# Shifting the SBUF pools of an attention and expert-layer kernel by 64 to 224 bytes

## The chip, the core and the metric

The kernel runs on one core of one Trainium2 chip. The metric is the device time of one execution in microseconds. Three timed runs of the kernel before gave 777.49, 779.59 and 781.82 us; their median, 779.59 us, is the time before.

## What is computed

Two steps follow each other. The first is block-sparse attention over 4 batches, 8 heads, 768 positions and head size 64: a query block of 32 positions sees its neighbours, the first and last block, and three sampled blocks; the first and last query blocks see all.

```python
scores = np.where(mask, scale * q @ k.T, -1e9)
attn = softmax(scores)              # over the keys
x = (attn @ v)                      # 3072 tokens x 512 features
h = x @ w_in                        # 512 -> 2048
g = s * np.maximum(h, 0) ** 2 + b
out = g @ w_out                     # 2048 -> 512
```

The weights arrive as 64-bit floats, and the two matrix products of the second step are done in three single-precision passes each (high by high, high by low, low by high), so that they come out in full precision.

## The kernel before, in words

**Attention.** 52 slots of work (44 for query blocks that see a window and three sampled blocks, 8 for the first and last blocks, which see all: the dense slots) are put in an order by a planner (class `Plan`), which simulates the engines with given costs; the order is then fixed in the program, and nothing is decided at run time apart from the addresses of sampled blocks. A slot runs through scores (lines 921 and 943), minimum and mask (960), exponential (972), transposes by TensorE (998 and 1000), their copies to SBUF (1011 on VectorE, 1013 on ScalarE), the products with the values (1042 and 1052), a scaling (1058), a transpose back (1064), a copy (1069) and a store to DRAM (1077). Keys `kt` are loaded at the start in pieces of 512 bytes per partition and block (692), values `vA` and `vB` in pieces of 2048 bytes (758 to 771 and 865), queries `qr` at line 706, on the queue of SyncE for dense slots and of GpSimd for the others.

**Decoding the weights.** Each 64-bit weight tile is split into a high and a low single-precision tile by nine steps on VectorE and ScalarE (lines 79 to 89). This runs beside the attention and the first part of the second step.

**Expert layer.** Groups of 384 tokens are taken one after the other. The first two groups use plain products (lines 432 to 434: 12 matmuls of 384 columns for each group of 128 hidden features). The other six go by Strassen's scheme, two groups at a time: line 611 issues six matmuls of 384 columns for each product, seven products in place of eight. The hidden values are squared, split into high and low (line 453 on GpSimd), and multiplied by `w_out` (lines 474 to 476: nine matmuls of 512 columns for each group of hidden features).

Every matmul has its own weight load. In lines 432 to 434 and 611 the weights come from the tiles `win` or `wop`, and the moving operand is `xp` (or a tile laid over `wout` or `win`). In lines 474 to 476 the weights are `hid` and the moving operand is `wout`, `woutr` or `win`.

**Where the tiles lie.** A tile pool is a stretch of each SBUF partition; pools that are opened one after the other lie one behind the other. From the bottom: `cpool` (constants), `kp` (`kt`, `kk`, `win`, `raw`, the work tiles of the decoding, the sums), `gp` (`vA`, `vB`, `wout`, `dp`, `xp`), `cp` (`ptile`, later `hid`), and above them the pools that attention alone uses (`pers`, `qp`, `ptp`, `sm` and another one named `xp`). When attention is over, the pool `wo` (`woutr`, `xrest`, `ob`) is laid over those. In `kp`, `gp` and `cp` every tile is a multiple of 512 bytes long, so that all of them have the same place modulo 512 in their partitions.

Of the kernel before, what the change touches and what calls it, by code (L numbers as in the profile page):

```python
# [9 lines left out]
F32 = mybir.dt.float32  # L10
# [9 lines left out]
P = 128  # L20
# [186 lines left out]
def kernel(  # L207
# [42 lines left out]
    cpool = ctx.enter_context(tc.tile_pool(name="cpool", bufs=1))  # L250
# [4 lines left out]
    b_top = cpool.tile([P, 1], F32, name="b_top")  # L255
    nc.gpsimd.memset(b_top, F32_MOST + F64_SHIFT)
    b_most = cpool.tile([P, 1], F32, name="b_most")
    nc.gpsimd.memset(b_most, F32_MOST)
    xd = dpool.tile([B // 2, 2, P, NM, 2, NPAIR, BLK], F32, name="xd")
    wod = dpool.tile([4, P, 2 * DM], F32, name="wod")  # L260
# [16 lines left out]

    gp = ctx.enter_context(tc.tile_pool(name="gp", bufs=2))
    cp = ctx.enter_context(tc.tile_pool(name="cp", bufs=1))

    ptiles = [cp.tile([P, HALF], F32, tag=f"p{n}", name=f"ptile{n}") for n in range(8)]
    ps = ctx.enter_context(tc.tile_pool(name="ps", bufs=1, space=PSUM))

# [18 lines left out]
    wts, wos, moved = {}, {}, {}  # L302
# [16 lines left out]
    def win_tile(k):  # L319
        if k not in wts:  # L320
            wts[k] = kbig(k, f"win{k}").rearrange("p n a c -> p (n a c)") if k < 2 else kp.tile([P, 14 * NW], F32R, tag="kk", name="win2", bufs=1)
        return wts[k]
# [11 lines left out]
    def wos_tile(k):  # L334
        if k not in wos:
            pair = wos[("pair", k // 2)] = gp.tile([P, 2, 4 * DM], F32R, tag="vg", name=f"wout{k}", bufs=2)
            wos[k // 2 * 2], wos[k // 2 * 2 + 1] = pair[:, 0], pair[:, 1]
        return wos[k]

    def wout(f, part):  # L340

        if f in moved:
            return moved[f][part]
        if f < 2:
            return win_tile(0)[:, (8 + 2 * f + part) * NW:(9 + 2 * f + part) * NW]
        if f < 8:
            o = (2 * (f % 2) + part) * DM
            return wos_tile(f // 2)[:, o:o + DM]
        if "rest" not in wos:
            es.close()  # L350
            wos["pool"] = ctx.enter_context(tc.tile_pool(name="wo", bufs=1))
            wos["rest"] = wos["pool"].tile([P, NFC - 9, 2, DM], F32R, name="woutr")
            wos["x"] = wos["pool"].tile([P, HALF], F32, name="xrest")
        if f == NFC - 1:
            return win_tile(2)[:, (10 + part) * NW:(11 + part) * NW]
        return wos["rest"][:, f - 8, part, :]
# [106 lines left out]
    def mlp2(i, gf=None):  # L463
        g, f = gf or subs[i]
        gh, gl = htile(2 + i % 3), htile(5 + i % 3)
        b, hf = divmod(g, 2)
        count[g] = count.get(g, 0) + 1
        first, last = count[g] == 1, count[g] == NFC
        for t in range(TG):
            if first:  # L470
                po[(g, t)] = bank(2 + 3 * hf + t, f"o{g}_{t}")
            acc = po[(g, t)]
            tsl = slice(t * P, (t + 1) * P)
            nc.tensor.matmul(acc, gh[:, tsl], wout(f, 0), start=first, stop=False)  # L474
            nc.tensor.matmul(acc, gh[:, tsl], wout(f, 1), start=False, stop=False)  # L475
            nc.tensor.matmul(acc, gl[:, tsl], wout(f, 0), start=False, stop=last)  # L476
            if last:
                ob = wos["pool"].tile([P, DM], F32, tag="ob", name=f"ob{g}_{t}", bufs=3)
                if t % 2 == 0 or b < B - 1:
                    nc.scalar.copy(ob, acc)  # L480
                else:
                    nc.vector.tensor_copy(ob, acc)
                tok = BLK + hf * G + t * P
                if tok + P <= S:
                    nc.sync.dma_start(out=out[b * S + tok:b * S + tok + P, :], in_=ob)
                else:
                    nc.sync.dma_start(out=out[b * S + tok:(b + 1) * S, :], in_=ob[:P - BLK])
                    nc.sync.dma_start(out=out[b * S:b * S + BLK, :], in_=ob[P - BLK:])
# [1060 lines left out]
```

## Time and profile before

| | |
|---|---|
| median of the three timed runs | 779.59 us |
| span of the profiled execution | 784.0 us |
| TensorE busy | 742.1 us, 95% |
| VectorE busy | 581.4 us, 74% |
| ScalarE busy | 472.9 us, 60% |
| GpSimd busy | 248.5 us, 32% |
| moved by DMA | 89.41 MB |

The profiled execution gives no other time of its own than its span, from its first to its last instruction. It lies 4.4 us above the median of the timed runs. Busy time is the sum over the instructions of an engine; a long busy time alone doesn't say that the engine sets the end, for that the chain of waits is read.

### The profile page before, as it was taken

What the parts mean: (1) busy time and instruction counts of PE and PEld (TensorE: products, weight loads), DVE (VectorE), ACT (ScalarE), POOL (GpSimd) and SP (SyncE); (2) the same over time, 40 slices, a digit from 0 to 9 for tenths busy, and PEclk for the clock granted to TensorE, in tenths of its full rate; (3) what the DMA queues carried; (4) which work ended last, traced back from release to release, by engine and by line L of the source; (5) the groups of instructions that cost most, each with busy time, mean ns of one, the idle gap of its engine ahead of it and who ended that gap; (6) DMA issues with size and microseconds to landing.
All of it is one profiled execution on the core that took longest, in us unless ns stands there. A gap on an engine that the chain in (4) does not pass through costs nothing.

```text
span 784.0 us, 21344 instructions
## 1 busy us (share of the span) xinstructions
PE 742.1 (95%) x8032; PEld 625.6 (80%) x8032; DVE 581.4 (74%) x1436; ACT 472.9 (60%) x1141; POOL 248.5 (32%) x395
## 2 busy tenths in 40 slices
PE   8899798998698999999989999999999999999997
PEld 6477675666576889988878888888889888989996
DVE  4657366888687699999898678787668678666652
ACT  3667476788587677778764344475554467445443
POOL 4746244434421232221322223232322223222321
PEclk9889899999899999999999999999999999999999
DMA  9978888756774544544632321125000022000002
GB/s 241 232 199 223 220 218 235 188 159 188 192 198 137 143 133 144 161 142 132 143 114 69 113 75 61 55 54 161 1 1 1 0 61 81 1 1 0 1 1 80
DMA packets 101110, 89.41 MB, mean 114 GB/s; under 512 B 50192, under 2 KB 79504, under 8 KB 101008
## 3 DMA queue, kind: packets, MB, share of 16 engines
q1 hardware_dynamic: 98704, 81.76, 37.2%
q0 software_dynamic: 2304, 6.29, 3.3%
q8 instruction: 63, 1.03, 0.6%
q14 instruction: 39, 0.32, 0.2%
HBM read 69.15 MB, written 14.68 MB: 107 GB/s over the span
## 4 chain that ended last, share of the span: by engine, by line
PE 66%; DVE 16%; ACT 5%; DMA 5%; issue 5%; SPq 2%; POOL 1%; ACTq 0%; POOLq 0%; DVEq 0%
PE m L611 21%; PE o L475 8%; PE o L476 8%; PE o L474 8%; PE s L943 6%; PE xs L1052 5%; PE t L1000 5%; DMA xd<-xst 2%; PE od L1042 2%; DVE win L89 1%; PE xs L1064 1%; DMA qr_3s<-in_q_dup_dram 1%; DVE wout L89 1%; DVE wkhp L88 1%; DVE wklp L82 1%
## 5 line engine op out<-in xcount | busy, mean ns | idle before, releaser
L453 POOL TENSOR_TENSOR hid<-hid,hid 128x384 fp32r<-128x384 f32 x122 | 134.7, 1105 | 369.5 <-ACT hid L629 269.1
L628 ACT ACTIVATE hid<-hid,sb_b,sb_s 128x384 f32<-128x384 f32 x96 | 68.0, 709 | 152.6 <-DVE hid L622 152.6
L972 ACT ACTIVATE ptile<-ptile,nm 128x256 f32<-128x256 f32 (+1 forms) x208 | 107.3, 518 | 44.1 <-DVE nm L960 43.7
L960 DVE CUSTOM_DVE_ANT_1 ptile<-s,mt 128x256 f32<-128x256 f32 x176 | 64.4, 421 | 35.2 <-PE s L943 34.1
L476 PE MATMUL o<-woutr,hid 128*128 128x512 f32 x168 | 66.4, 395 | 0.0
L475 PE MATMUL o<-woutr,hid 128*128 128x512 f32 x168 | 66.3, 395 | 0.0
L611 PE MATMUL m<-wout,win 128*128 128x384 f32 x264 | 62.8, 342 | 3.0 <-ACT xrest L1442 3.0
L474 PE MATMUL o<-woutr,hid 128*128 128x512 f32 x168 | 65.3, 389 | 0.0
L611 PE MATMUL m<-xp,wop 128*128 128x384 f32 x288 | 59.2, 341 | 0.0
L1000 PE MATMUL t<-ident,ptile 128*128 128x128 f32 x352 | 53.0, 296 | 4.9 <-issue 4.8
L1052 PEld LDWEIGHTS xs<-vA,pt 128*32 128x32 f32 x1696 | 36.0, 114 | 26.3 <-issue 10.5
L475 PE MATMUL o<-win,hid 128*128 128x512 f32 x144 | 56.8, 394 | 0.0
L622 DVE SCALAR_TENSOR_TENSOR hid<-hid 128x384 f32<-128x384 f32 x96 | 54.2, 564 | 3.3
L611 PE MATMUL m<-xp,win 128*128 128x384 f32 x288 | 54.8, 337 | 1.2 <-DVE sum L1451 0.8
L1052 PE MATMUL xs<-vA,pt 128*32 128x64 f32 x1696 | 48.1, 228 | 6.5 <-issue 6.3
L611 PEld LDWEIGHTS m<-xp,wop 128*128 128x128 f32 x288 | 52.3, 191 | 2.1
L611 PEld LDWEIGHTS m<-xp,win 128*128 128x128 f32 x288 | 51.0, 188 | 3.8 <-issue 1.1
L629 ACT CAST hid<-hid 128x384 fp32r<-128x384 f32 x96 | 49.4, 515 | 7.3
L882 POOL COPY kk<-kt 128x256 f32<-128x256 f32 (+2 forms) x46 | 20.6, 451 | 104.2 <-PE s L943 104.2
L611 PEld LDWEIGHTS m<-wout,win 128*128 128x128 f32 x264 | 47.8, 189 | 5.7 <-ACT xrest L1442 3.9
L476 PE MATMUL o<-win,hid 128*128 128x512 f32 x126 | 49.9, 396 | 1.7 <-POOL hid L453 1.7
L1000 PEld LDWEIGHTS t<-ident,ptile 128*128 128x128 f32 x352 | 41.0, 149 | 12.1 <-issue 6.3
(188 smaller groups left out, 1867.9 us busy)
## 6 DMA issues: line engine op xcount, KB each, us to landing
vB<-in_v_dram SPq DMA_DIRECT2D x109, 128.0 KB, 3.9
vA<-in_v_dram SPq DMA_DIRECT2D x72, 128.0 KB, 4.1
raw_o<-in_w_out_dram SPq DMA_DIRECT2D x14, 512.0 KB, 3.3
raw_i<-in_w_in_dram SPq DMA_DIRECT2D x12, 512.0 KB, 3.8
xd<-xst SPq DMA_DIRECT2D x44, 128.0 KB, 3.6
out_dram<-ob SPq DMA_DIRECT2D x20, 256.0 KB, 2.0
sum<-xd SPq DMA_DIRECT2D x12, 384.0 KB, 4.4
kt<-in_k_blk_dram SPq DMA_DIRECT2D x8, 384.0 KB, 5.6
```

The lines of the kernel that those rows point to most:

```text
L453: (eng or nc.vector).tensor_tensor(out=htile(5 + i % 3), in0=t, in1=gh.bitcast(F32), op=ALU.subtract)
L474: nc.tensor.matmul(acc, gh[:, tsl], wout(f, 0), start=first, stop=False)
L475: nc.tensor.matmul(acc, gh[:, tsl], wout(f, 1), start=False, stop=False)
L476: nc.tensor.matmul(acc, gl[:, tsl], wout(f, 0), start=False, stop=last)
L611: nc.tensor.matmul(to, w_, x_, start=(c == 0 and k == 0), stop=(c == 1 and k == 2))
L622: vec.scalar_tensor_tensor(out=t, in0=t, scalar=0.0, in1=t, op0=ALU.max, op1=ALU.mult)
L628: nc.scalar.activation(t, t, AF.Identity, bias=sb_b, scale=sb_s)
L629: nc.scalar.copy(gh, t)
L960: nc.vector.tensor_tensor_reduce(out=pt, in0=sp, in1=msk, scale=-scale, scalar=FMAX if g == 0 else nm[:, 0:1], op0=ALU.add, op1=ALU.min, a ...
L972: nc.scalar.activation(pt[:, :w], pt[:, :w], AF.Exp, bias=nms[n][:, last:last + 1], scale=-1.0, accum_out=dns[i][:, g, j:j + 1])
L1000: nc.tensor.transpose(tp[:, (2 * j + c) * P:(2 * j + c + 1) * P], src[:, c * P:(c + 1) * P], ident)
L1052: nc.tensor.matmul(xs[quads[pair]], pt[:, c, quads[pair]], vt[:, a, col:col + D], start=(j == 0 and c == 0), stop=(c == 1), tile_position= ...
```

## The change

Three small tiles are allocated that no instruction writes or reads. One of 64 bytes per partition closes `cpool`, one of 64 bytes opens `gp`, one of 96 bytes opens `wo`.

```diff
@@ -255,6 +255,7 @@
     b_top = cpool.tile([P, 1], F32, name="b_top")
     nc.gpsimd.memset(b_top, F32_MOST + F64_SHIFT)
     b_most = cpool.tile([P, 1], F32, name="b_most")
+    cpool.tile([P, 16], F32, name="shift0")
     nc.gpsimd.memset(b_most, F32_MOST)
@@ -277,7 +278,7 @@
     gp = ctx.enter_context(tc.tile_pool(name="gp", bufs=2))
     cp = ctx.enter_context(tc.tile_pool(name="cp", bufs=1))
-
+    gp.tile([P, 16], F32, name="shift1", bufs=1)
     ptiles = [cp.tile([P, HALF], F32, tag=f"p{n}", name=f"ptile{n}") for n in range(8)]
@@ -349,6 +350,7 @@
             wos["pool"] = ctx.enter_context(tc.tile_pool(name="wo", bufs=1))
+            wos["pool"].tile([P, 24], F32, name="shift3")
             wos["rest"] = wos["pool"].tile([P, NFC - 9, 2, DM], F32R, name="woutr")
```

On every engine the same instructions stand in the same order as before, with the same waits; their addresses in SBUF alone differ. Addresses in PSUM and DRAM stay. The places of the tiles in their partitions, in bytes modulo 512:

| tiles (pool) | before | after | moved by |
|---|---|---|---|
| `kt`, `kk`, `win`, `raw`, `wkhp`, `wklp`, `sum`, `wop` (`kp`) | 256 | 320 | 64 |
| `vA`, `vB`, `wout`, `dp`, `xp` (`gp`) | 256 | 384 | 128 |
| `ptile`, `hid` (`cp`) | 256 | 384 | 128 |
| `ident` (`pers`) | 256 | 384 | 128 |
| `qr` (`qp`), `pt` (`ptp`), `xss`, `xst` (`xp`) | 192 | 320 | 128 |
| `mz` / `mt` (`pers`) | 480 / 224 | 96 / 352 | 128 |
| `woutr`, `xrest`, `ob` (`wo`) | 256 | 480 | 224 |

So the weights `win` and the moving `xp`, which had the same place before, are now 64 bytes apart, and the weights `hid` and the moving `woutr` 96 bytes; `hid` and `wout` still have the same place.

## Rows read from the trace of the kernel before

**Rows 1.** Stages: from:to us, length, busy us (instructions) by engine, clock, DMA share, GB/s.
```profile
0.00:50.00 50.00, 44.41 (x524) 29.88 (x524) 27.51 (x99) 26.49 (x79) 30.26 (x82) 0.86 0.93 225
...
100.00:200.00 100.00, 91.38 (x2340) 65.05 (x2339) 78.27 (x297) 76.13 (x241) 46.05 (x106) 0.97 0.74 200
...
300.00:400.00 100.00, 96.22 (x471) 86.22 (x471) 94.44 (x151) 77.28 (x141) 23.36 (x19) 0.98 0.48 144
...
500.00:600.00 100.00, 99.81 (x496) 89.55 (x495) 74.58 (x149) 56.34 (x116) 28.67 (x26) 1.00 0.18 49
...
700.00:784.00 84.00, 78.89 (x388) 70.02 (x386) 46.00 (x96) 34.57 (x71) 20.07 (x20) 0.99 0.05 20
```

**Rows 2.** The chain that ended last, shares of the span by engine and by line.
```profile
PE 66%; DVE 16%; ACT 5%; DMA 5%; issue 5%; SPq 2%; POOL 1%; ACTq 0%; POOLq 0%; DVEq 0%
PE m L611 21%; PE o L475 8%; PE o L476 8%; PE o L474 8%; PE s L943 6%; PE xs L1052 5%; PE t L1000 5%; DMA xd<-xst 2%; PE od L1042 2%; DVE win L89 1%; PE xs L1064 1%; DMA qr_3s<-in_q_dup_dram 1%; DVE wout L89 1%; DVE wkhp L88 1%; DVE wklp L82 1%
```

**Rows 3.** Timeline of TensorE from 560.7 us: start, length, matmuls merged by line.
```profile
560.74 1.23 PE L611 MATMUL m<-xp,wop 128*128 128x384 f32 x6
561.81 0.39 PE L474 MATMUL o<-woutr,hid 128*128 128x512 f32 x1
...
563.89 2.26 PE L611 MATMUL m<-xp,win 128*128 128x384 f32 x12
565.99 0.39 PE L474 MATMUL o<-wout,hid 128*128 128x512 f32 x1
```

**Rows 4.** The same view at 377.6 us, where 512-column matmuls follow one another.
```profile
377.59 0.39 PE L474 MATMUL o<-woutr,hid 128*128 128x512 f32 x1
...
379.63 0.39 PE L474 MATMUL o<-woutr,hid 128*128 128x512 f32 x1
```

**Rows 5.** Whole span, matmuls and weight loads of lines 611, 474 and 432, in this order.
```profile
0.00:784.00 784.00, 195.00 (x1008) 180.52 (x1008) 0.98 0.41 114
...
0.00:784.00 784.00, 149.60 (x384) 72.30 (x384) 0.98 0.41 114
...
0.00:784.00 784.00, 43.60 (x128) 24.04 (x128) 0.98 0.41 114
```

**Rows 6.** Groups by form: line, engine, out<-in, shapes, count | busy us, mean ns | idle before.
```profile
L1000 PE MATMUL t<-ident,ptile 128*128 128x128 f32 x352 | 53.0, 296 | 4.9 <-issue 4.8
...
L1011 DVE COPY pt<-t 128x512 f32<-128x512 f32 x44 | 30.1, 683 | 10.3 <-PE t L1000 9.8
L1013 ACT COPY pt<-t 128x512 f32<-128x512 f32 x44 | 25.7, 585 | 21.9 <-PE t L1000 21.9
...
L1064 PE MATMUL xs<-ident,xss 128*128 128x128 f32 x88 | 18.5, 293 | 6.0 <-DVE xss L1058 6.0
...
L480 ACT COPY ob<-o 128x512 f32<-128x512 f32 x22 | 12.1, 588 | 7.3 <-PE o L476 5.7 <-DMA out_dram<-ob 1.2
...
L482 DVE COPY ob<-o 128x512 f32<-128x512 f32 x2 | 1.4, 691 | 6.4 <-PE o L476 4.3 <-DMA out_dram<-ob 2.2
```

**Rows 7.** Line 611 at 564.06 and 564.59 us: duration ns min/median/max, first and last start.
```profile
L611 PE MATMUL m<-xp,win x2: 333/336/339, 563.9 to 564.1; 128*128 128x384 f32 x2
...
L611 PE MATMUL m<-xp,win x2: 339/341/343, 564.4 to 564.6; 128*128 128x384 f32 x2
```

**Rows 8.** Single microseconds at the start, columns as in group 1.
```profile
5.00:6.00 1.00, 1.00 (x6) 1.00 (x6) 0.84 (x4) 0.00 (x0) 0.78 (x2) 1.00 1.15 347
...
8.00:9.00 1.00, 1.00 (x11) 1.00 (x10) 0.00 (x0) 0.00 (x0) 0.78 (x3) 1.00 1.09 306
...
13.00:14.00 1.00, 0.81 (x6) 0.22 (x4) 0.85 (x5) 1.00 (x5) 0.00 (x0) 1.00 1.14 344
```

**Rows 9.** Line 89 of the decoding: duration ns min/median/max, first and last start.
```profile
L89 DVE SCALAR_TENSOR_TENSOR win<-wklp,wkhp x17: 691/693/1526, 145.9 to 384.0; 128x512 fp32r<-128x512 f32 x17
L89 DVE SCALAR_TENSOR_TENSOR wout<-wklp,wkhp x8: 693/1392/1523, 272.0 to 315.0; 128x512 fp32r<-128x512 f32 x8
L89 DVE SCALAR_TENSOR_TENSOR woutr<-wklp,wkhp x7: 691/1382/1533, 323.9 to 377.7; 128x512 fp32r<-128x512 f32 x7
```

## The prediction

> **What bounds the kernel now.** I read the stages first. In the first 50 us the DMA engines are busy 0.93 of the time and no other engine is full; from 100 us on TensorE is, with 91 of 100 us, later 96 and 99.8; between 300 and 400 us VectorE stands beside it with 94.44 of 100 [rows 1]. The chain of waits says the same in shares: TensorE holds 66% of it, VectorE 16%, ScalarE 5%, DMA 5%, and of TensorE's part line 611 and lines 474 to 476 make 45 points [rows 2]. So the kernel is bound by TensorE's pace in its second two thirds, by VectorE's decoding in part of the middle, and by transfers at the start. Nothing idles there that a shorter wait could fill. A change of places can move the time only if one of these three runs at another pace at another place.
>
> **What the change removes, adds and moves.** No instruction is added, removed or moved on any queue, and no wait. The term "instructions" of the sum is 0 us. Left is one term for each engine: its instructions at the new places against the old ones. The trace never shows the big tiles at 320, 384 or 480 modulo 512, so each term is bounded by operations that it shows at two other places, 192 and 256, one of them off the 256-byte grid.
>
> ScalarE: the copy of 128x512 numbers from PSUM takes 585 ns into `pt` (at 192) and 588 ns into `ob` (at 256) [rows 6]. The difference is 3 of 588 ns, 0.5%, in either direction. On ScalarE's 5% of the chain, 39 us of 784, that is ±0.2 us.
>
> VectorE: the same copy takes 683 ns into `pt` and 691 ns into `ob` (two instances only) [rows 6], 1.2%. On 16% of the chain, 125 us, that is ±1.5 us; I take 0, because 44 instances against two are no measured difference.
>
> TensorE in attention: a transpose of 128x128 takes 296 ns with its weights in `ptile` (at 256) and 293 ns with them in `xss` (at 192) [rows 6]. The moving operand is `ident` both times, so the distance between the two operands' places is 0 in one case and 64 bytes in the other, the distance that `win` and `xp` get. That is 1%, but these matmuls are short and of another kind than those below, and a conflict could hide in them.
>
> TensorE in the expert layer, the term that matters. In some products the low part of the moving operand is read in runs of 128 bytes with a step of 256, the first half of it from place 256 on, the second from 384 on. Each of the two rows holds one of them and the matmul still running before it. At 564.06 us the first kind starts and is the longer of its row, 339 ns; at 564.59 us the second starts and is the shorter, 339 ns [rows 7]. So a moving operand that starts at 384 and touches other places than its weights goes at the same pace as one that starts at 256. I take 0 for the whole term, since this is the nearest row: same line, same type, same columns.
>
> Its bounds come from the pace itself. Nine matmuls of 512 columns take 563.89 - 561.81 = 2.08 us when they follow a product of line 611 [rows 3], and 379.63 - 377.59 = 2.04 us when they follow others of their kind [rows 4]. A product of six matmuls of 384 columns takes 561.81 - 560.74 = 1.07 us after such a run, two in a row 565.99 - 563.89 = 2.10 us [rows 3], so the second takes 1.03. After each change of kind the pace is thus 0.04 us lower for one group. If that is a conflict between weight loads and moving reads, and it vanishes, the gain is 3 x 384 / 9 = 128 runs of nine (three lines of equal count) times 0.04 = 5.1 us; and for 1008 / 6 = 168 products, half of them first in a row, and 128 / 4 = 32 groups of the plain products, 116 in all, times 0.04 = 4.6 us [rows 3 to 5]. Together 9.7 us is the bound below. A bound much further down: in 2.04 us for nine, one matmul takes 226.7 ns, while 512 columns at the granted clock of 1.00, that is 2.4 GHz, need 213.3; if the 13.3 ns were conflict too, on 1008 + 3 x 384 + 3 x 128 = 2544 matmuls [rows 5] they are 34 us. Bound above: every first group's delay also strikes the other 84 products (3.4 us), and the runs of nine lose as much again as they do now (5.1 us): 8.5 us.
>
> What the Trainium skill says here. "TensorE: Matmul & The Clock Gate", section "Step-by-step: what each phase is for", gives TensorE two independent read ports, so that loading the next weights takes nothing from the running matmul; by it the term is 0 wherever the tiles lie, and the time 779.6 us, as I take it. The same page, section "Back-to-back issue gap", gives N/2.4 + 2.5 ns, 215.8 ns for 512 columns; the trace has 226.7 [rows 4] and differs, so 10.9 ns for each matmul are without an explanation, some 28 us over 2544, and the two-port rule isn't proved by this case.
>
> GpSimd: nothing shows it at another place. It is busy 20 to 30 of 100 us from 300 us on [rows 1] and 1% of the chain [rows 2], so a few per cent of its pace cost nothing; it counts only through VectorE (below).
>
> DMA: queries `qr` land at place 192, keys at 256, both in pieces of 512 bytes. Pure key traffic runs at 347 GB/s between 5 and 6 us; with the order of issue, the queries fall roughly into 8 to 9 us and 13 to 14 us, where 306 and 344 GB/s pass [rows 8]. Against the higher one the loss is 1%, against the lower one 12%. DMA's 5% of the chain is 39 us, so 0.4 to 4.7 us. I take 0, the nearer row being the second, where no key load is left to mix in. A gain would need the grid of 192 to be better than that of 256, which no row shows.
>
> Sum: 0 + 0 + 0 + 0 + 0 us on the profiled execution's 784.0 us. That one lies 4.4 us above the median of the timed runs, so the forecast is set on the median: 779.59 + 0, rounded to 779.5 us. Runs of before differ by ±2.2 us, so about 0.5%, 3.9 us, is what can be told from no change.
>
> **The rivals.**
>
> *TensorE gets smoother.* All operands of a matmul start at the same place modulo 512 now, and after the change `win` and `xp` are 64 bytes apart, `hid` and `woutr` 96. If the 0.04 us for each change of kind come from both reads meeting in one place, they go. For it speaks that the delay is regular and no other engine is named as its cause; against it the two 339 ns [rows 7], and that the delay is absent in rows 4 at unchanged distances. Price: 9.7 us less what VectorE's 94% between 300 and 400 us hides, about a sixth: -8 us, 771.5 us.
>
> *TensorE gets rougher.* The same mechanism turned round: today's equal places keep the two reads out of step, and 64 bytes bring them together. The place is the second product in a row and every run of nine, the price up to 8.5 us: 788 us. It decides from 1.5 ns for each of the 2544 matmuls on (3.9 us). It has the same evidence against it, and rows 4 show that a run at equal places can be free of the delay, so there is something to lose.
>
> *Transfers into SBUF get slower.* Destinations move off the 256-byte grid (320 and 384). With the 12% of rows 8 on DMA's 39 us of the chain the time is +4.7, 784.3 us. It decides from 10% on. Beside it stands the page "DMA: Bandwidth & Descriptors", section "How a descriptor splits into AXI transactions": a descriptor that doesn't start on 256 bytes costs beats for the part before its start. By it pieces of 512 bytes at 320 would take 18 beats for 16, those of 2048 at 384 would take 68 for 64. The 344 GB/s of rows 8 for pieces at 192 don't bear it out, the 306 might.
>
> *VectorE and GpSimd meet otherwise.* Line 89 takes 691 to 693 ns alone, and up to 1533 [rows 9]. Over 693 ns the eight with a median of 1392 hold 8 x 0.70 = 5.6 us, the seven with 1382 hold 7 x 0.69 = 4.8, and of the 17 with a median of 693 fewer than half can hold up to 0.83 each, 0 to 6.7: 10.4 to 17.1 in all, about 13. If small shifts of phase change which of them meet GpSimd's line 453, half of it comes or goes, ±6.5 us: 773 or 786 us. Against it: nothing shifts the phase unless another term isn't 0.
>
> **How the numbers follow.** No change: 0.50. Smoother TensorE: 0.29. Rougher: 0.09. Slower transfers: 0.07. Another phase: 0.05, half to either side. Faster by over 0.5% is 0.29 + 0.02 = 0.31, slower 0.09 + 0.07 + 0.03 = 0.19, within 0.5% 0.50. The evidence for no change comes from neighbouring places, not from the new ones, which is why half is left to the others, and more of it below, where the removable 13.3 ns lie. The likeliest case alone spans 775.7 to 783.5 us. The range reaches past the smoother case in full (779.6 - 9.7 = 770) to 768, which takes in a little of the 34 us, and above to 787, short of the rougher case's end: 768 to 787 us.
>
> **What would show it.** Right: runs of nine at 2.08 and 2.04 us, products at 1.07 and 1.03, copies at 585 to 588 and 683 to 691 ns, and 340 to 350 GB/s between 5 and 8 us. Smoother or rougher would show in the same two timeline views first, long before the stages; slower transfers in the first 50 us, as a later first product with the values; another phase in the durations of line 89 alone. The forecast is wrong if TensorE's stage from 500 to 600 us, 496 matmuls in 100 us now [rows 1], holds 3 matmuls more or fewer.

## The result and the profile after

The changed kernel is slower: 786.81 us median (783.23 to 790.63, 12 runs) against 781.05 for the kernel before, timed beside it (777.49 to 783.22, 12 runs). The medians lie 5.8 us apart; the ratio is 1.0082, 95% interval 1.0057 to 1.0107. A second series gave 787.65 (7 runs) against 781.79, ratio 1.0120 [1.0083, 1.0157]. The ratios here and below are taken from the runs of the chip's faster state and not from the medians; two of the twelve runs of `v_first` are left out as slow. The forecast was 779.5 and no change.

The two profiled executions don't show it in their spans: 784.1 us after, 784.0 before. That one of before was among its kernel's slowest; TensorE stands still once for 4.3 us at 206 us, and over the stretch from 204 to 221 us every other execution profiled here is 2 to 5 us quicker. So the timed runs decide how much, and the profile is read for where. The chain of before has (start, length, released by):

```profile
205.99 4.34 issue
```

The stages of after, with single microseconds behind them; columns are those of [rows 1]:

```profile
0.00:50.00 50.00, 38.30 (x406) 25.89 (x410) 24.50 (x88) 23.33 (x69) 27.85 (x77) 0.84 0.96 208
100.00:200.00 100.00, 91.81 (x2421) 65.66 (x2406) 80.27 (x304) 77.24 (x247) 46.66 (x109) 0.98 0.78 205
...
500.00:600.00 100.00, 99.82 (x496) 89.35 (x495) 74.04 (x148) 56.21 (x117) 29.18 (x27) 1.00 0.21 49
...
5.00:6.00 1.00, 1.00 (x6) 1.00 (x6) 0.83 (x4) 0.00 (x0) 0.78 (x2) 1.00 1.15 329
8.00:9.00 1.00, 1.00 (x11) 1.00 (x10) 0.00 (x0) 0.00 (x0) 0.78 (x3) 1.00 1.18 280
13.00:14.00 1.00, 1.00 (x16) 0.61 (x12) 0.85 (x3) 0.00 (x0) 0.00 (x0) 0.73 1.17 290
```

In the first 50 us the DMA engines are busier than before (0.96 for 0.93) and move less (208 GB/s for 225): 10.4 MB for 11.25. The missing 0.85 MB are 4.1 us at 208 GB/s, and TensorE gets through 406 matmuls for 524 [rows 1]. That is one execution: the second profile of the same kernel has 217 GB/s and 548 matmuls in these 50 us, so neither the 4.1 us nor the 406 measures the kernel. The rate of the loads while keys pass is what returns in every profile (below). At 13 us the DMA engines move 290 GB/s for 344 [rows 8]. The stage from 500 to 600 us is as it was, 496 matmuls.

The time from issue to landing (last column, us) in the first 40 us, first before, then after:

```profile
kt<-in_k_blk_dram SPq DMA_DIRECT2D x8, 384.0 KB, 5.6
...
qr_0d<-in_q_edge_dram SPq DMA_DIRECT2D x4, 128.0 KB, 5.1
qr_4s<-in_q_dup_dram POOLq DMA_DIRECT2D x4, 128.0 KB, 7.0
```
```profile
kt<-in_k_blk_dram SPq DMA_DIRECT2D x8, 384.0 KB, 6.8
...
qr_0d<-in_q_edge_dram SPq DMA_DIRECT2D x4, 128.0 KB, 6.4
qr_4s<-in_q_dup_dram POOLq DMA_DIRECT2D x4, 128.0 KB, 9.1
```

Keys and queries land 1.2 to 2.1 us later. The first 25 us of before, v_qr, v_128, after and after_again (v_qr and v_128 are described in the next section; in the first two kernels the keys lie on 256 bytes, in the others off them):

```profile
0.00:25.00 25.00, 22.22 (x172) 17.13 (x176) 13.66 (x45) 12.62 (x34) 14.86 (x47) 1.00 0.95 240
0.00:25.00 25.00, 20.35 (x156) 15.74 (x156) 13.11 (x42) 11.52 (x31) 14.86 (x47) 0.93 0.95 244
0.00:25.00 25.00, 20.13 (x145) 15.30 (x146) 11.30 (x37) 10.31 (x27) 14.78 (x47) 0.86 0.99 213
0.00:25.00 25.00, 20.24 (x145) 14.97 (x146) 11.30 (x37) 10.28 (x27) 14.88 (x47) 0.93 0.98 213
0.00:25.00 25.00, 20.13 (x148) 15.13 (x149) 11.59 (x37) 10.46 (x29) 14.87 (x47) 0.93 0.98 217
```

From 5 to 8 us, before and after:

```profile
5.00:8.00 3.00, 3.00 (x17) 3.00 (x17) 0.84 (x4) 0.00 (x0) 2.41 (x7) 1.00 1.15 346
5.00:8.00 3.00, 3.00 (x21) 3.00 (x21) 0.83 (x4) 0.00 (x0) 2.41 (x7) 1.00 1.16 303
```

TensorE's expert layer does change its cadence, but in both directions. The timeline of after at the places of [rows 3], then of [rows 4]:

```profile
560.30 1.20 PE L613 MATMUL m<-xp,wop 128*128 128x384 f32 x6
561.34 0.39 PE L476 MATMUL o<-woutr,hid 128*128 128x512 f32 x1
...
563.45 2.26 PE L613 MATMUL m<-xp,win 128*128 128x384 f32 x12
565.54 0.40 PE L476 MATMUL o<-wout,hid 128*128 128x512 f32 x1
```
```profile
375.93 0.39 PE L476 MATMUL o<-woutr,hid 128*128 128x512 f32 x1
...
378.03 0.39 PE L476 MATMUL o<-woutr,hid 128*128 128x512 f32 x1
```

Six matmuls after a run of nine take 561.34 - 560.30 = 1.04 us for 1.07, nine after a product 563.45 - 561.34 = 2.11 for 2.08, nine after their kind 378.03 - 375.93 = 2.10 for 2.04.

### The profile page after: what moved, and what is told of

It reads as the page before. It is cut to its first block, busy times and chain, and to the rows that moved or that the text cites. A ratio compares the mean times of both kernels' runs of the same rounds, so it can differ in the third digit from the quotient of the medians.

```text
span 784.1 us, 21344 instructions
## 1 busy us (share of the span) xinstructions
PE 737.6 (94%) x8032; PEld 623.0 (79%) x8032; DVE 582.1 (74%) x1436; ACT 472.7 (60%) x1141; POOL 249.0 (32%) x395
## 4 chain that ended last, share of the span: by engine, by line
PE 78%; issue 6%; DMA 5%; DVE 4%; POOL 3%; ACT 3%; SPq 1%; POOLq 0%; ACTq 0%; DVEq 0%
PE m L613 21%; PE o L476 11%; PE o L478 11%; PE o L477 11%; PE xs L1054 5%; PE s L945 4%; PE t L1002 4%; PE h L434 3%; PE h L435 3%; PE h L436 3%; PE od L1044 2%; DMA qr_3s<-in_q_dup_dram 1%; POOL kk L895 1%; PE xs L1066 1%; DVE whole L580 1%
## 5 line engine op out<-in xcount | busy, mean ns | idle before, releaser
L477 PE MATMUL o<-win,hid 128*128 128x512 f32 x144 | 57.0, 396 | 0.0
L478 PE MATMUL o<-win,hid 128*128 128x512 f32 x126 | 50.0, 397 | 1.0 <-POOL hid L455 1.0
L476 PE MATMUL o<-win,hid 128*128 128x512 f32 x126 | 49.8, 395 | 0.3 <-ACT ob L482 0.2
```

## The experiments

**Two benches of places.** The first loads into one tile at chosen places (its core: `t = big[:, off // 4:...]`, then the DMAs of keys, values and queries); the second runs the expert layer's groups of six and nine matmuls from tiles at chosen places.

> Computes nothing: it only loads into one tile at chosen places modulo 512 bytes, one stretch for each place, and writes zeros. Keys come in pieces of 512 bytes (places 256, 256, 0, 32, ... 480, and 256, 320, 192, 0 again), pairs of keys in pieces of 1024, values in pieces of 2048, queries in pieces of 512 into 64 partitions at a time, then stores. Theory 'destinations off a grid are slower': keys pass at 340 to 350 GB/s at places 0 and 256, as the profile of before has them, and at about 290 at 320, as the profile of after has them; the places between tell which grid it is (64, 128 or 256 bytes); pieces of 2048 lose a quarter as much as those of 512, 4 to 5%. By the page on descriptors the loss at 320 would be 18 beats for 16, 340 to 303. Rival 'the slow start has another cause' (more transfers in flight at once, another order of arrival): all places pass at the same rate within 3%.

A stretch from the middle of each: place 0, 32, 224, 320 with pieces of 512 bytes, then 0 and 192 with pieces of 1024 (columns after from:to: length, VectorE, GpSimd, clock, DMA share, GB/s):

```profile
31.00:38.00 7.00, 0.93 (x6) 0.00 (x0) 1.00 1.14 342
41.00:48.00 7.00, 0.84 (x6) 0.00 (x0) 1.00 1.14 288
105.00:112.00 7.00, 0.84 (x6) 0.00 (x0) 1.00 1.21 290
128.00:135.00 7.00, 0.81 (x6) 0.00 (x0) 1.00 1.16 290
...
231.00:237.00 6.00, 0.46 (x3) 0.00 (x0) 1.00 1.09 386
258.00:264.00 6.00, 0.46 (x3) 0.00 (x0) 1.00 1.09 348
```

It is a step, not a slope: on the 256-byte grid (0 and 256) 332 to 345 GB/s and 27.1 to 27.4 ns for a piece of 512 bytes, at each of the thirteen places off it 288 to 292 GB/s and 31 to 34 ns, 32 and 64 bytes off as much as 128 or 224. Pieces of 1024 take 46.0 ns on the grid and 50 to 52 off it. Queries alone through SyncE's queue, 64 partitions at a time, pass at 195 to 216 GB/s everywhere, and don't care. In the Trainium skill, page "DMA: Bandwidth & Descriptors", section "How a descriptor splits into AXI transactions", a descriptor off the grid pays for the bytes between the boundary and its start, which are fetched and not used. Worked out from that as an estimate, a piece of 512 takes 17 beats for 16 at 32 and 23 for 16 at 224. Here it is the destination that is off the grid; the direction agrees, the amount doesn't: both places cost the same 18 to 19% in time.

> Computes nothing of use: groups of six matmuls of 384 columns and runs of nine of 512, in the expert layer's order (six, six, nine), from tiles that lie at chosen places; first weights at 256 and moving operand at 256 plus 0, 32, ... 480, then both at 0, 64, 128, 192, then the places of before (all 256) and of after (320 and 384 for the products, 384 and 480 for the runs of nine). Theory 'the pace depends on the distance of the two operands': after a run of nine the first six take 1.065 us at distance 0 and 1.045 at 64, nine take 2.08 us at distance 0 and 2.10 at 96, and the numbers repeat by distance, not by the places themselves. Rival 'the pace does not depend on places': all stretches agree within 0.003 us for each group.

TensorE's timeline at distance 0, then at distance 64 (start, length, merged by line):

```profile
63.74 2.24 PE L259 MATMUL bank<-xbig,wbig 128*128 128x512 f32 x9
65.83 2.27 PE L251 MATMUL bank<-xbig,wbig 128*128 128x384 f32 x12
67.93 2.24 PE L259 MATMUL bank<-xbig,wbig 128*128 128x512 f32 x9
```
```profile
97.30 2.22 PE L259 MATMUL bank<-xbig,wbig 128*128 128x512 f32 x9
99.36 2.24 PE L251 MATMUL bank<-xbig,wbig 128*128 128x384 f32 x12
101.44 2.22 PE L259 MATMUL bank<-xbig,wbig 128*128 128x512 f32 x9
```

Nine take 2.081 us at distance 0 (moving less weights) and 2.060 at 64; the first six of twelve 1.066 and 1.040. At 32 and from 96 to 224 nine take 2.087 to 2.106. All repeats after 256 bytes, and with distance 0 it is the same at 0, 64, 128, 192, 256 and 320: the distance counts, not the place. With the places of the changed kernel the first six take 1.037, nine 2.098. The theory held; of its numbers 1.045 was too high. But a group's own distance isn't all. In one stretch the products keep their distance of 0 and only the runs of nine get 96:

```profile
534.66 2.24 PE L251 MATMUL bank<-xbig,wbig 128*128 128x384 f32 x12
536.74 2.26 PE L259 MATMUL bank<-xbig,wbig 128*128 128x512 f32 x9
538.84 0.33 PE L251 MATMUL bank<-xbig,wbig 128*128 128x384 f32 x1
```

The twelve take 2.08 us for the 2.10 beside runs at distance 0, their first six 1.040 for 1.066. Turned round, runs at 0 beside products at 64 take 2.076 for 2.081. So the neighbours' places count too.

**Parts of the change, and its terms kept apart.** All these kernels have the instructions of before, one for one; only places differ. The edits, each on the kernel before:

```
v_first      after b_most:  cpool.tile([P, 16], F32, name="shift0")
v_second     after gp:      gp.tile([P, 16], F32, name="shift1", bufs=1)
v_128        after b_most:  cpool.tile([P, 32], F32, name="shift0")
v_grid       after vA, vB:  gp.tile([P, 16], F32, name="apart", bufs=1);  wo: [P, 24] first
v_qr         after ident:   pers.tile([P, 16], F32, name="shift2")
v_apart      cp made ahead of gp;  after vA, vB: gp.tile([P, 16], F32, name="apart", bufs=1)
v_apart_128  v_apart and v_128 together
v_best       cp, kk, khp, klp behind sb_b; then b_top, b_most, the rest; shift2
```

> Only the first of the three small tiles: everything moves by 64 bytes, so that keys, values, win, hid and wout lie at 320, the queries at 256, and the operands of a matmul keep their distance of 0. Theory 'transfers' (keys at 320 cost the 5 us of the first 50): pure key traffic at 290 GB/s, ratio of after to before 1.004 to 1.007; TensorE's groups as before (1.066, 2.08 us). Rival 'TensorE's pace is the whole loss': ratio 1.000 within 0.002. Rival 'phase': anything from 0.992 to 1.008 with transfers and groups as before.

> Only the second small tile: keys and win stay at 256, values, xp, hid and wout move to 320, queries to 256. Theory 'transfers': keys at 346 GB/s, values of 2048 bytes 4% slower, ratio 1.000 to 1.002. On TensorE the products get a distance of 64 and should take 1.045 us after a run of nine instead of 1.066 (about -2 us over the expert layer), the runs of nine keep their distance of 0 and 2.08 us: so 0.996 to 1.000 in all. Rival 'TensorE's pace is the whole loss': 0.997 and no change in the first 50 us.

> One small tile of 128 bytes at the front instead of the three: every place moves by 128 bytes, keys, values, win, hid and wout to 384, the queries to 320; the two operands of a matmul keep their distance of 0. All loads of the start are off the 256-byte grid, TensorE's pace is as before. Theory 'transfers': keys pass at 290 GB/s, the whole loss of the change is there: ratio 1.004 to 1.008. Rival 'half transfers, half TensorE': ratio 1.002 to 1.004, as the kernel with the first small tile alone (1.0012) plus what the queries add. Rival 'TensorE's pace': 1.000 within 0.002.

> The counterpart: keys, win and values at 256 and the queries at 256, so that every load of the start lies on the 256-byte grid; xp, dp and hid at 320 and woutr at 416, so that TensorE's operands stand as far from one another as after the change or nearly (moving less weights 64 in most products, -64 or 96 in the runs of nine). Theory 'transfers': no loss in the first 50 us, ratio 0.999 to 1.002. Rival 'half and half': 1.003 to 1.004. Rival 'TensorE's pace is the whole loss': 1.006 to 1.009.

> One tile of 64 bytes behind ident alone: queries, pt, xss and xst move from 192 to 256, all else stays where it was before. So every load of the start is on the 256-byte grid and TensorE is as before. Theory 'the grid decides, for the queries too' (before had them off it): the kernel gains what the counterpart with all loads on the grid gained (0.9958), ratio 0.994 to 0.998. Rival 'queries lose nothing off the grid' (they land in 64 partitions, and the bench of places had them at 200 GB/s everywhere): 1.000 within 0.002, and the counterpart's gain came from TensorE's distances.

> The changed kernel once more, on the chip and beside the runs of before that the other three share: ratio 1.0057 to 1.0107 as the first time if its loss belongs to the kernel and not to the chip it ran on; 1.001 to 1.003 if it was the chip.

What they gave, in the order of how much of the start is off the grid. "TensorE" is how much longer than in before the stretch from the matmul that starts at 428 us in before to the last one takes, from the starts in the timeline:

```
kernel       off the grid            median / before   ratio [95%]               TensorE us
v_qr         nothing                 779.13 / 782.96   0.9962 [0.9929, 0.9994]    0.00
v_grid       nothing                 778.39 / 781.79   0.9958 [0.9932, 0.9984]   +0.08
v_second     values                  780.71 / 781.81   0.9982 [0.9962, 1.0003]   -0.79
before       queries                                   1
v_first      keys, values            784.35 / 781.81   1.0012 [0.9981, 1.0044]   +0.01
v_128        keys, values, queries   786.44 / 781.79   1.0053 [1.0024, 1.0082]    0.00
after        keys, values, queries   786.81 / 781.05   1.0082 [1.0057, 1.0107]   +0.60
after_again  keys, values, queries   787.65 / 781.79   1.0120 [1.0083, 1.0157]   +0.58
```

The two ends are far apart: v_128 loses 0.5% with TensorE exactly as before, v_grid, with TensorE's distances near those of after, wins 0.4%. So the loss is the loads'. The busy times of the other engines grow by less than it in v_128: VectorE 584.3 us for 581.4, ScalarE 473.1 for 472.9, GpSimd 248.7 for 248.5. From 5 to 8 us, where keys alone pass, the six profiles with keys on the grid have 345 to 347 GB/s, the five with keys off it 301 to 309. TensorE's matmul that starts at 100 us in before's profile comes 3.7 to 5.1 us earlier in the four kernels with every load on the grid (with v_apart and v_best of below), and between 1.5 us earlier and 3.2 us later in the five with keys off it; these are single executions. v_qr shows what I had not seen at all: the kernel before already paid some 3 us (interval 0.5 to 5.6), most likely because its queries lay at 192; `pt`, `xss` and `xst` moved with them, and no run keeps these apart. Steps between neighbours are within their intervals, so the order in the table is not shown step by step; the ends are far outside them.

Several expectations were missed. v_first gave 1.0012 where 1.004 to 1.007 stood; its queries come onto the grid, which fits giving back what keys and values lose, but its interval reaches to 1.0044. v_grid gave 0.9958 where 0.999 to 1.002 stood, because the gain of the queries was not reckoned with, and after_again 1.0120, above 1.0057 to 1.0107. v_second gained 0.79 us on TensorE and not 2: 31 of its runs of nine read `win`, which lies 64 bytes below `hid` there, and take 2.103 us for 2.087. That after is a little above v_128 is +0.6 us of TensorE and within the intervals for the rest.

The same microsecond, 13 to 14 us, in v_128 and in v_qr:

```profile
13.00:14.00 1.00, 1.00 (x12) 0.75 (x8) 0.41 (x1) 0.00 (x0) 0.00 (x0) 0.50 1.19 288
```
```profile
13.00:14.00 1.00, 1.00 (x12) 0.69 (x6) 0.83 (x3) 0.16 (x1) 0.00 (x0) 0.50 1.15 348
```

**Queries and keys at once.**

> Computes nothing: queries through GpSimd's software queue alone at 256, 256, 192, 320, 0, 256; then queries and keys (SyncE's queue) at the same time at (keys, queries) = (256, 256), (256, 192), (320, 256), (320, 320), twice; then values in pieces of 2048 bytes, 6.3 MB each, at 256, 320, 384, twice. Theory 'off the grid each piece of 512 bytes takes the engines 19% longer wherever it lands': together with keys, a section of 5.8 MB takes 17 us at (256, 256), 18.5 at (256, 192), 18.7 at (320, 256) and 20 at (320, 320); values 4 to 30% slower off the grid. Rival 'queries are bound by something else': (256, 192) takes as long as (256, 256) within 2%.

Half a miss. Queries through the software queue alone take 11.9 to 12.2 us at 256, 10.9 at 0, 13.5 at 192 and 13.2 at 320, their 4096-byte packets 214 to 252 ns on the grid and 300 or more off it. Beside keys the two sections of each kind take 19.7 and 22.0 us at (256, 256), 20.7 and 21.1 at (256, 192), 19.6 and 24.2 at (320, 256), 23.3 and 23.8 at (320, 320). Two sections of one kind differ by up to 4.6 us, and in the first of (256, 256) the keys had landed before the queries were issued; so at most the last kind stands out, and (256, 192) isn't told from (256, 256). GpSimd takes 616 ns on the mean for each issue, some 12 us for the 20 of a section, which is too slow for a bound. Values in pieces of 2048, at 256 and at 320:

```profile
275.00:284.00 9.00, 2.12 (x15) 0.00 (x0) 1.00 1.05 406
290.00:299.00 9.00, 2.15 (x14) 0.00 (x0) 1.00 1.05 387
```

They lose 5%; the 20 to 30% that the shorter sections of the first bench seemed to show don't hold over a longer one.

**A version that beats both.**

> A version meant to be faster than before: hid's and the probabilities' pool lies ahead of the values' and a small tile of 64 bytes between the values and xp. Keys, win, values, hid at 256, queries on 256, xp at 320, woutr at 320. By the bench of places, six matmuls after a run of nine take 1.040 us at a distance of 64 for 1.066 at 0, and nine take 2.060 for 2.081. Four of seven products read xp (116 first groups times 4/7 times 0.026 = 1.7 us) and seven of sixteen runs of nine read woutr (128 times 7/16 times 0.021 = 1.2 us): -3 us, and up to -1 more for the queries: ratio 0.995 to 0.997. If the pace of TensorE isn't what is late there: 0.999 to 1.001.

> The version with xp and woutr 64 bytes off their partners, and everything 128 bytes further: all distances as in that version, all loads of the start off the grid (keys, values, queries at 384). Theory 'two separate terms': the loss of the kernel moved by 128 (1.0053) on top of that version's TensorE gain (3 us, 0.996): ratio 1.000 to 1.003, and the cadence of that version: nine in 2.060 us with woutr. If that version's gain came from the loads alone: 1.004 to 1.006; if from TensorE alone: 0.990 to 0.994.

> Every load of the start on the 256-byte grid (keys, values, queries at 256, raw at 256) and a distance of 64 (moving less weights, modulo 256) wherever the memory allows it without a byte more than before: hid, kk, wop, whole at 192, all others at 0 or 256. By the benches: nine matmuls with any wout but the one in kk take 2.060 us for 2.081 (128 times 15/16 times 0.021 = 2.5 us), four products of seven are free of the 0.026 us (116 times 4/7 times 0.026 = 1.7 us), and the loads give the 0.4% of the kernel with the queries alone moved (0.9962): -7 us, ratio 0.988 to 0.993; between 428 and 778 us of before TensorE gains 3.5 to 4.5 us, more than the 3.1 of the version with xp and woutr apart. If TensorE's distances were not additive to the loads: 0.994 to 0.997.

v_apart: 775.24 us against 781.79, ratio 0.9909 [0.9878, 0.9940], better than expected. v_best: 775.63 against 781.39, 0.9925 [0.9896, 0.9955]; v_apart_128: 780.71 against 782.96, 0.9971 [0.9941, 1.0000], a little under the 1.000 to 1.003 expected. Between v_apart and v_apart_128 lie the loads alone (0.6%), with TensorE at -3.15 us from 428 us on in both: the two terms add up within the intervals. v_apart's timeline:

```profile
551.92 1.20 PE L610 MATMUL m<-xp,wop 128*128 128x384 f32 x6
552.96 0.39 PE L473 MATMUL o<-woutr,hid 128*128 128x512 f32 x1
...
555.02 2.25 PE L610 MATMUL m<-xp,win 128*128 128x384 f32 x12
557.11 0.39 PE L473 MATMUL o<-wout,hid 128*128 128x512 f32 x1
```

Nine take 2.06 us. v_best, with the distance of 64 at more places, gains only 2.60 us there, not 3.5 to 4.5, and isn't told from v_apart by its time. Over the same stretch its runs of nine take 2.066 us on the mean and v_apart's 2.061, though in v_apart wout outside woutr still has the distance 0. So the bench's rule by one matmul's own distance does not carry over whole. The neighbours' places count too, as the bench shows, but its 2.076 us for runs at 0 beside products at 64 doesn't give these numbers, and how they count stays open.

## Why the prediction was wrong

*Instructions, ScalarE, VectorE.* Right at 0. The copies of after:

```profile
L1013 DVE COPY pt<-t 128x512 f32<-128x512 f32 x44 | 30.1, 684 | 8.7 <-PE t L1002 8.4
L1015 ACT COPY pt<-t 128x512 f32<-128x512 f32 x44 | 25.7, 583 | 22.6 <-PE t L1002 22.5
```

684 and 583 ns for 683 and 585 [rows 6]. `pt` lies off the grid before and after; on it, in v_qr, the copies take 684 and 584 ns. The copies into `ob`, which moves from 256 to 480, take 692 and 587 ns for 691 and 588. Off the grid or on it, these copies take the same time.

*GpSimd and VectorE meeting otherwise.* Nothing came of it; line 89's groups are as in [rows 9]:

```profile
L89 DVE SCALAR_TENSOR_TENSOR wout<-wklp,wkhp x8: 693/1397/1525, 270.4 to 313.4; 128x512 fp32r<-128x512 f32 x8
L89 DVE SCALAR_TENSOR_TENSOR woutr<-wklp,wkhp x7: 691/1386/1526, 322.3 to 376.0; 128x512 fp32r<-128x512 f32 x7
```

*TensorE in the expert layer.* Forecast 0, measured +0.6 us from 428 us on, inside the bounds -9.7 and +8.5. The reason was wrong. The two reads of 339 ns [rows 7] are lengths of single matmuls, which overlap; the cadence is in the steps from start to start, and these differ by place. It came out near 0 because two effects nearly cancel: over that stretch the first six after a run of nine went from 1.062 to 1.048 us (87 of them, -1.2 us), the second six from 1.054 to 1.060 (65, +0.4), nine from 2.083 to 2.098 (87, +1.3). Not all of the nine go up: with `wout` they take 2.078 for 2.081, with `woutr` 2.103 for 2.082 and with `win` 2.103 for 2.087. The section on the change had left out that `win`, where it is the moving operand, comes to lie 64 bytes below `hid`. "Smoother" and "rougher" were both right, each for one kind of group, and both prices were too high, as bounds are: the products gained 1.2 us of at most 4.6, the runs of nine lost 1.3 of at most 5.1, and v_apart gets 3.15 us of the 9.7. That the term came out near its 0 is luck.

*DMA, the step that failed.* The term was put at 0, and v_128, with TensorE as before, measures it: 0.53% (0.24 to 0.82), some 4.1 us. The prediction took 0 because "the nearer row" of queries at 192 was 13 to 14 us with 344 GB/s. That microsecond holds no queries: the pieces of 512 bytes in it take 27.0 ns each, as those of the keys do from 5 to 8 us, and the last keys land at 15.8 us, the next queries at 16.6. The queries were guessed into it by the order of issue; their own row was the other one, 8 to 9 us with 306 GB/s, where qr_0d passes among the keys. Read so, the loss at 192 was up to 12% of the rate (v_qr, with the queries on the grid, has 329 GB/s in that microsecond, so not all of it is the place), and the bench gives 15% (342 to 290). The rival "Transfers into SBUF get slower" had the mechanism, the place and nearly the price (+4.7 us; +5.8 came, of which TensorE has 0.6), but a chance of 0.07. The price was near by luck: it scaled DMA's 5% of the chain with a microsecond that mixes keys and queries. The sentence "A gain would need the grid of 192 to be better than that of 256" shows the same blind spot: the queries of the kernel before were off the grid already, so a new row of theirs could not clear the shift.

*The check named.* The stage from 500 to 600 us, with three matmuls more or fewer as the sign of a miss, came out at 496 and would have called the forecast right. It watched the wrong stage. The other sign, 340 to 350 GB/s between 5 and 8 us, shows it at once: 303 after.

## What to carry over

Where a kernel starts bound by transfers, put every tile that DMAs fill in small pieces on a 256-byte grid, and look at where a pool's small tiles push those behind them: 64 bytes cost 15% of the rate here. For back-to-back matmuls the distance of the two operands modulo 256 was worth a percent here. And before a rate is used as evidence for a tile, see in the trace that this tile's packets passed in that stretch.

## What was not expected of the hardware

- The rate of loads has two levels, by whether the destination starts on 256 bytes: 27.1 and 31 to 34 ns for 512 bytes, 46.0 and 50 to 52 for 1024, 84.0 and 87.4 for 2048; how far off the grid plays no part in the rate (288 to 292 GB/s at all thirteen places).
- TensorE's matmuls of 512 columns with weights loaded for each take 228.9 ns on the mean in a run of nine at a distance of 64 (2.060 / 9), 231.2 at 0 and up to 234 elsewhere, at the clock of 1.00 all the while; the pattern repeats after 256 bytes, and the distance in the neighbouring groups changes it (1.040 for 1.066 us in six matmuls of 384 columns whose own places stayed).
